# Float32r weights that begin 192 instead of 64 bytes past multiples of 256

## The chip, the cores and the metric

The kernel runs on one core of one Trainium2 chip. The metric is the device time of one execution in microseconds; less is better. A core has five engines with queues of their own: TensorE (PE in the profile; its weight loads are listed as PEld), VectorE (DVE), ScalarE (ACT), GpSimd (POOL) and SyncE (SP), which here only issues DMAs. On-chip memory (SBUF) has 128 partitions; "address" in this document always means the byte address within a partition, and "at 64" means that an operand begins 64 bytes past a multiple of 256.

## The reference

The input `x` is 8 x 3136 x 256. The reference takes the real part of a two-dimensional Fourier transform over the last two axes and puts a feed-forward block with a residual behind it:

```python
X = np.fft.fft(x, axis=1)
X = np.fft.fft(X, axis=2)
x = X.real.astype(np.float32)

mu = np.mean(x, axis=-1, keepdims=True)
var = np.mean((x - mu) ** 2, axis=-1, keepdims=True)
xn = (x - mu) / np.sqrt(var + 1e-06) * g_ln
ch = np.maximum(xn @ w_ch1, 0.0) @ w_ch2      # 256 -> 1024 -> 256
return (x + ch).astype(np.float32)
```

All data are float32.

## The kernel before

**The transform.** The sequence axis (3136 = 49 x 64) is transformed in two steps. `step1` (L247) multiplies folded input with a 64-point table; its result goes to a scratch buffer in device memory and comes back in another order (`store1`, `relayout`). `step2` (L299) multiplies the result, as weights, with tables `tab_s` as moving operand (L309, plain float32) and writes the pieces `ckh` and `ckl` of a chunk of 256 tokens (L330, L334). The transform over the last axis is folded into the first weight matrix, `w1`; only for the residual is it done explicitly (`residual`, L422, with weights from `ck` and the moving table `ty_s`, L428, plain float32).

**The feed-forward block.** It works chunk by chunk (`NCH` = 49 of them), and each chunk in eight steps of 128 hidden features. Step `s` has three parts, written out in this order in the main loop (L813 on): `moe1_b(s - 1)` makes the hidden activations' two pieces, `moe1_a(s)` the next hidden features, `moe2(s - 3)` adds the output of an earlier step.

**Products in three passes.** A float32 product is made of float32r products, which TensorE streams at one column a cycle: each operand is split into a high piece, rounded to float32r, and the rest. `PASSES` (L337) names the three products that count: high x low, low x high, high x high. `moe1_a` (L354) takes slices of `w1_hi` and `w1_lo` as weights (the stationary operand, 128 columns, loaded by a weight load ahead of each product) and `ckh`, `ckl` as moving operand (256 columns). `moe2` (L404) takes slices of `h_hi` and `h_lo` as weights and `w2_hi`, `w2_lo` as moving operand (256 columns). From the second batch on `step1` does the same with `t1_hi`, `t1_lo` as weights and `f_hi`, `f_lo` as moving operand (L262, 512 columns).

So one step of the loop is 6 products of `moe1_a` and 12 of `moe2`, each with a weight load of its own. TensorE can load the next weights while a product streams. Other products (L309, L428, L262, some small ones) come between steps, where the lists `after` and `late` (L606) put them. The order on TensorE, ScalarE, VectorE and GpSimd is that of the program text.

**Where operands lie.** Tiles get their addresses from pools, one after the other, in the order of the pools and of their tiles. The first pools are:

```python
moving.tile([128, 32], F32, name="margin")
w2_hi = moving.tile([128, 8, D], F32R, name="w2_hi")
w2_lo = moving.tile([128, 8, D], F32R, name="w2_lo")
weights.tile([128, 16], F32, name="offset")
w1_hi = weights.tile([128, 2, FF], F32R, name="w1_hi")
w1_lo = weights.tile([128, 2, FF], F32R, name="w1_lo")
```

`moving` holds the moving operands of all float32r products: `w2_hi`, `w2_lo`, `f_hi`, `f_lo`, `ck_hi`, `ck_lo`. Its tile `margin` is never used; it fills up to a multiple of 256 bytes, and the tiles behind it are multiples of 256 bytes long, so all of them begin at 0. `weights` holds the weights of float32r products (`w1_hi`, `w1_lo`, `t1_hi`, `t1_lo`, `h_hi`, `h_lo`) and two kinds of tiles that are weights of plain float32 products, `s2` (L309) and `ck` (L428). Its first tile, `offset`, isn't used either: its 16 elements make the rest begin at 64. These tiles too are multiples of 256 bytes long (`h_hi` and `ck` have 2304 bytes, 9 x 256), and the slices that become weights begin at multiples of 512 bytes within them. Exceptions: the second half of `ck` begins 1152 bytes into its tile, and one slice in the last chunk at element 120. Behind `weights` come the pools `const` (tables, the input `xs`) and `work` (everything that VectorE, ScalarE and GpSimd pass on); each start there is rounded up to 32 bytes.

Of the kernel before, what the change touches and what calls it, by code (L numbers as in the profile page):

```python
# [20 lines left out]
F32 = mybir.dt.float32  # L21
# [125 lines left out]
def tile_kernel(ctx: ExitStack, tc: tile.TileContext, x, g_ln, w1, w2, tu, tab, tz, ty, tw, out):  # L147
    nc = tc.nc
    moving = ctx.enter_context(tc.tile_pool(name="moving", bufs=1))
    weights = ctx.enter_context(tc.tile_pool(name="weights", bufs=1))  # L150
# [5 lines left out]
    moving.tile([128, 32], F32, name="margin")  # L156
    w2_hi = moving.tile([128, 8, D], F32R, name="w2_hi")
    w2_lo = moving.tile([128, 8, D], F32R, name="w2_lo")
    weights.tile([128, 16], F32, name="offset")
    w1_hi = weights.tile([128, 2, FF], F32R, name="w1_hi")  # L160
    w1_lo = weights.tile([128, 2, FF], F32R, name="w1_lo")
    t1_hi = weights.tile([128, 128], F32R, name="t1_hi")
# [683 lines left out]
```

## Time and profile before

| | us |
|---|---|
| median of 3 runs | 1007.62 (1007.08 to 1007.76) |
| the profiled execution | 1007.27 |
| its span, first to last instruction | 1005.5 |
| TensorE matmuls, busy | 995.1 |
| VectorE, busy | 812.3 |
| ScalarE, busy | 540.1 |
| GpSimd, busy | 243.9 |

The profile is of one execution. In its groups, a row gives line, engine, operation, output tile and input tiles, shapes and count; behind the bar stand busy time in us, the mean of one instruction in ns, and the idle time before these instructions with what ended it. Matmuls overlap: the next one starts long before the one before it has ended, so the sum of their durations isn't the time that they take, and the distance from start to start has to be read from the timeline. A row of the timeline gives the start in us from the span's start, the length in us, and the instruction. A row of the windows gives a stretch, its length, then busy time and number of instructions for PE, PEld, DVE, ACT and POOL, the granted clock, the DMA engines' share and GB/s.

### The profile page before, as it was taken

To read this page: it belongs to the slowest core of one execution; us is meant where nothing else is said; L and a number is where in the kernel's file an instruction comes from. 1 tells how busy PE (TensorE), PEld (TensorE's weight loads), DVE (VectorE), ACT (ScalarE), POOL (GpSimd) and SP (SyncE) were. 2 spreads that over 40 slices of the span, in tenths; PEclk is the share of its full clock that TensorE was granted. 3 is DMA by queue.
4 is the path that set the end of the run, shared out by engine and by line. 5 is a ranking of instruction groups with operands and counts; after the bars stand their busy time and mean duration, and the time that the engine had idled before them with its cause. 6 is when DMAs were issued, how large, how long until landed. Compare 5 with 4: busy or idle time off the path is not lost.

```text
span 1005.5 us, 21770 instructions
## 1 busy us (share of the span) xinstructions
PE 995.1 (99%) x8289; PEld 973.7 (97%) x8289; DVE 812.3 (81%) x2190; ACT 540.1 (54%) x1416; POOL 243.9 (24%) x278
## 2 busy tenths in 40 slices
PE   9999999999999999999999999999999999999998
PEld 6799999999999999999999999999999999999998
DVE  7788887878787788878877887878788788887887
ACT  3655556554555555655456555555555554555553
POOL 2146414530153203440054401532034300000000
PEclk9999999999999999999999999999999999999999
DMA  9933243223122511333132232224101230100101
GB/s 346 266 141 126 85 143 110 86 84 108 62 95 85 157 44 53 103 120 105 44 111 101 74 106 75 84 96 126 55 32 44 74 105 23 43 22 22 43 22 43
DMA packets 41528, 92.10 MB, mean 92 GB/s; under 512 B 4176, under 2 KB 18704, under 8 KB 40528
## 3 DMA queue, kind: packets, MB, share of 16 engines
q1 hardware_dynamic: 40016, 88.87, 27.1%
q8 instruction: 66, 1.08, 0.5%
q0 software_dynamic: 320, 1.05, 0.3%
q10 hardware_dynamic: 1088, 0.79, 0.2%
q14 instruction: 38, 0.31, 0.1%
HBM read 50.32 MB, written 40.37 MB: 90 GB/s over the span
## 4 chain that ended last, share of the span: by engine, by line
PE 88%; DVE 7%; ACT 2%; DMA 2%; issue 1%; SPq 0%; ACTq 0%; DVEq 0%
PE acc L404 49%; PE ab L354 25%; PE ps L309 5%; PE psy L428 4%; PE ps L262 3%; DVE h_lo L369 2%; DVE h L360 1%; DVE h L361 1%; ACT h_hi L368 1%; PE ps L255 1%; PE ps L257 1%; DMA scratch<-s 1%; DMA s<-scratch 1%; DMA xs<-x 0%; DVE st L450 0%
## 5 line engine op out<-in xcount | busy, mean ns | idle before, releaser
L404 PE MATMUL acc<-w_hi,h_lo 128*128 128x256 f32 x1568 | 437.1, 279 | 0.2 <-DVE h_lo L369 0.2
L404 PE MATMUL acc<-w_hi,h_hi 128*128 128x256 f32 x1568 | 436.9, 279 | 0.0
L404 PE MATMUL acc<-w_lo,h_hi 128*128 128x256 f32 x1568 | 436.9, 279 | 0.0
L369 DVE SCALAR_TENSOR_TENSOR h_lo<-h,h_hi 128x512 fp32r<-128x512 f32 x392 | 285.9, 729 | 160.8 <-ACT h_hi L368 159.0
L368 ACT ACTIVATE h_hi<-h 128x512 fp32r<-128x512 f32 x392 | 250.1, 638 | 266.0 <-DVE h L361 265.5
L404 PEld LDWEIGHTS acc<-w_hi,h_hi 128*128 128x128 f32 x1568 | 296.7, 189 | 0.0
L404 PEld LDWEIGHTS acc<-w_lo,h_hi 128*128 128x128 f32 x1568 | 295.3, 188 | 0.0
L404 PEld LDWEIGHTS acc<-w_hi,h_lo 128*128 128x128 f32 x1568 | 294.6, 188 | 0.6 <-DVE h_lo L369 0.4
L354 PE MATMUL ab<-ckl,w_hi 128*128 128x256 f32 x768 | 219.9, 286 | 2.6 <-DVE h L361 2.5
L354 PE MATMUL ab<-ckh,w_lo 128*128 128x256 f32 x768 | 214.5, 279 | 0.5 <-ACT ckh L330 0.3
L354 PE MATMUL ab<-ckh,w_hi 128*128 128x256 f32 x768 | 214.1, 279 | 0.0
L225 POOL TENSOR_TENSOR fl<-f,fh 128x512 fp32r<-128x512 f32 x49 | 64.2, 1309 | 495.5 <-ACT fh L219 489.3
L360 DVE TENSOR_TENSOR h<-asb,ab 128x256 f32<-128x256 f32 x384 | 158.7, 413 | 1.5 <-ACT asb L359 1.5
L361 DVE TENSOR_TENSOR h<-asb,ab 128x256 f32<-128x256 f32 x384 | 158.8, 414 | 0.0
L354 PEld LDWEIGHTS ab<-ckl,w_hi 128*128 128x128 f32 x768 | 144.3, 188 | 6.5 <-issue 2.1
L359 ACT COPY asb<-ab 128x256 f32<-128x256 f32 x384 | 139.0, 362 | 17.6 <-PE ab L354 13.9
L354 PEld LDWEIGHTS ab<-ckh,w_lo 128*128 128x128 f32 x768 | 144.7, 188 | 3.1 <-ACT ckh L330 0.5
L354 PEld LDWEIGHTS ab<-ckh,w_hi 128*128 128x128 f32 x768 | 145.3, 189 | 0.0
L330 ACT CAST ckh<-ps 128x392 fp32r<-128x392 f32 (+49 forms) x112 | 39.8, 356 | 62.3 <-PE ps L309 62.1
L265 ACT COPY s<-ps 128x508 f32<-128x508 f32 x56 | 32.8, 585 | 71.9 <-PE ps L262 58.7
L309 PE MATMUL ps<-tab_s,s 112*128 112x98 f32 (+1 forms) x512 | 65.6, 273 | 0.6 <-DMA s<-scratch 0.6
L309 PEld LDWEIGHTS ps<-tab_s,s 112*128 112x128 f32 x512 | 61.9, 191 | 1.1 <-PE pw L670 1.1
(108 smaller groups left out, 964.8 us busy)
## 6 DMA issues: line engine op xcount, KB each, us to landing
xs<-x SPq DMA_DIRECT2D x56, 512.0 KB, 4.4
out<-o SPq DMA_DIRECT2D x96, 256.0 KB, 3.0
scratch<-s SPq DMA_DIRECT2D x49, 256.0 KB, 2.2
s<-scratch SPq DMA_DIRECT2D x7, 1792.0 KB, 9.7
w1p_all<-w SPq DMA_DIRECT2D x8, 512.0 KB, 8.7
scratch<-s POOLq DMA_DIRECT2D x4, 256.0 KB, 6.3
s<-scratch SPq DMA_DIRECT2D x2, 448.0 KB, 5.8
s<-scratch SPq DMA_DIRECT2D x1, 896.0 KB, 12.2
```

What stands on the lines that cost most here:

```text
L225: nc.gpsimd.tensor_tensor(out=lo, in0=f, in1=hi.bitcast(F32), op=ALU.subtract)
L265: nc.scalar.copy(s[:, :, :, :127], ps[:, :, :, :127])
L309: nc.tensor.matmul(ps[:, h, k0 - base:k1 - base], s2[b][:KP, g, 128 * h:128 * h + 128], tab_s[:, h, k0:k1], start=(h == 0 and g == 2 * j), ...
L330: nc.scalar.copy(hi, src)
L354: nc.tensor.matmul(pt, wt[wi][:, j, fs], ch[xi][:, j, :w], start=(n == 0), stop=(n == 2))
L359: nc.scalar.copy(asb[:, :w], pa)
L360: nc.vector.tensor_tensor(out=h[:, :w], in0=asb[:, :w], in1=pb, op=ALU.add)
L361: nc.vector.tensor_tensor(out=h[:, w:], in0=asb[:, :m], in1=pb[:, :m], op=ALU.subtract)
L368: nc.scalar.activation(h_hi, h, AF.Relu)
L369: nc.vector.scalar_tensor_tensor(out=h_lo, in0=h, scalar=0.0, in1=h_hi.bitcast(F32), op0=ALU.max, op1=ALU.subtract)
L404: nc.tensor.matmul(acc[c, i][:, side], hs[xi][:, h0:h0 + 128], ws[wi][:, f], start=(f == 0 and side == 0 and n == 0), stop=(f == 7 and n = ...
L428: nc.tensor.matmul(ps[:, j, :129 + j], ck[:, j], ty_s[:, j, :129 + j], start=(j == 0), stop=True, skip_group_check=True)
```

## The change

The unused first tile of the pool `weights` grows from 16 to 48 elements, from 64 to 192 bytes. Every tile behind it moves up by 128 bytes: those of `weights`, `const` and `work`. The pool `moving` lies ahead of it and stays. So the weights of float32r products begin at 192 instead of 64 while their moving operands stay at 0; instructions, their order, waits and transfers are the same.

```diff
     w2_lo = moving.tile([128, 8, D], F32R, name="w2_lo")
-    weights.tile([128, 16], F32, name="offset")
+    weights.tile([128, 48], F32, name="offset")
     w1_hi = weights.tile([128, 2, FF], F32R, name="w1_hi")
```

## The prediction

> **What bounds the kernel now.** I read the page from the top: busy times, the clock row, the chain that ended last, then the groups of TensorE.
>
> ```profile
> span 1005.5 us, 21770 instructions
> ## 1 busy us (share of the span) xinstructions
> PE 995.1 (99%) x8289; PEld 973.7 (97%) x8289; DVE 812.3 (81%) x2190; ACT 540.1 (54%) x1416; POOL 243.9 (24%) x278
> ...
> PEclk9999999999999999999999999999999999999999
> ...
> PE 88%; DVE 7%; ACT 2%; DMA 2%; issue 1%; SPq 0%; ACTq 0%; DVEq 0%
> ```
>
> TensorE is busy for 99% of the span at the full granted clock, and 88% of the chain is its matmuls. Nothing else is close, so the time is the number of products times the distance from one to the next, plus the little that is left. What counts are the float32r products of `moe2` (L404) and `moe1_a` (L354):
>
> ```profile
> L404 PE MATMUL acc<-w_hi,h_lo 128*128 128x256 f32 x1568 | 437.1, 279 | 0.2 <-DVE h_lo L369 0.2
> L404 PE MATMUL acc<-w_hi,h_hi 128*128 128x256 f32 x1568 | 436.9, 279 | 0.0
> L404 PE MATMUL acc<-w_lo,h_hi 128*128 128x256 f32 x1568 | 436.9, 279 | 0.0
> ...
> L354 PE MATMUL ab<-ckl,w_hi 128*128 128x256 f32 x768 | 219.9, 286 | 2.6 <-DVE h L361 2.5
> L354 PE MATMUL ab<-ckh,w_lo 128*128 128x256 f32 x768 | 214.5, 279 | 0.5 <-ACT ckh L330 0.3
> L354 PE MATMUL ab<-ckh,w_hi 128*128 128x256 f32 x768 | 214.1, 279 | 0.0
> ```
>
> That is 4704 + 2304 = 7008 products of 256 columns. Their 279 ns is a mean of overlapping instructions, so the distance has to come from start times, and those show that 279 is no product's time. The timeline of TensorE has long unbroken stretches, of two kinds. First and last product of one stretch of each kind, with the groups and windows inside them:
>
> ```profile
> 233.69 0.28 PE L354 MATMUL ab<-ckh,w_lo 128*128 128x256 f32 x1
> ...
> 250.41 0.28 PE L404 MATMUL acc<-w_hi,h_hi 128*128 128x256 f32 x1
> ```
>
> ```profile
> 252.68 0.28 PE L354 MATMUL ab<-ckl,w_hi 128*128 128x256 f32 x1
> ...
> 268.54 0.28 PE L404 MATMUL acc<-w_hi,h_hi 128*128 128x256 f32 x1
> ```
>
> ```profile
> L404 PE MATMUL acc<-w_hi,h_lo 128*128 128x256 f32 x31 | 8.7, 281 | 0.0
> ...
> L404 PEld LDWEIGHTS acc<-w_hi,h_hi 128*128 128x128 f32 x31 | 6.0, 192 | 0.0
> L404 PEld LDWEIGHTS acc<-w_hi,h_lo 128*128 128x128 f32 x31 | 5.8, 188 | 0.0
> ```
>
> ```profile
> L404 PE MATMUL acc<-w_hi,h_lo 128*128 128x256 f32 x31 | 8.6, 276 | 0.0
> ...
> L404 PEld LDWEIGHTS acc<-w_hi,h_lo 128*128 128x128 f32 x31 | 5.8, 188 | 0.0
> ```
>
> ```profile
> 234.00:250.00 16.00, 16.00 (x138) 16.00 (x137) 14.42 (x41) 8.37 (x21) 0.00 (x0) 1.00 0.06 23
> 253.00:268.00 15.00, 15.00 (x135) 15.00 (x134) 13.67 (x40) 8.03 (x21) 0.95 (x1) 1.00 0.05 20
> ```
>
> From 233.69 to 250.41 lie 142 steps: 16.72 / 142 = **117.7 ns**. From 252.68 to 268.54 lie 140: 15.86 / 140 = **113.3 ns**. Same instructions, same addresses, clock 1.00, no idle time in either. In the slow stretch every product takes 281 ns and every third weight load 192; in the fast one they take 276 and 188. So each stretch runs in one of two rhythms, 4.4 ns apart, and the mean of 279 says how often: with 437.0 / 1568 = 278.7 ns, L404 is slow in (278.7 - 276) / (281 - 276) = 0.54 of its products. I take 0.54 for L354 too (its last two rows, 279.3 and 278.8, give 0.66 and 0.56, restarts included). That makes 3780 slow and 3230 fast products.
>
> What switches the rhythm is another kind of product in between, such as the three of L262, 512 columns wide. Here it goes from 113 to 118 ns:
>
> ```profile
> 206.67 0.28 PE L404 MATMUL acc<-w_lo,h_hi 128*128 128x256 f32 x1
> 206.78 0.28 PE L404 MATMUL acc<-w_hi,h_hi 128*128 128x256 f32 x1
> 206.90 0.39 PE L262 MATMUL ps<-fl,t_hi 128*128 128x512 f32 x1
> ...
> 207.71 0.28 PE L354 MATMUL ab<-ckh,w_lo 128*128 128x256 f32 x1
> 207.83 0.28 PE L354 MATMUL ab<-ckh,w_hi 128*128 128x256 f32 x1
> 207.94 0.28 PE L354 MATMUL ab<-ckl,w_hi 128*128 128x256 f32 x1
> 208.06 0.28 PE L354 MATMUL ab<-ckh,w_lo 128*128 128x256 f32 x1
> ```
>
> **The change, part by part.** It adds no instruction, wait or transfer and takes none away. Everything from `w1_hi` on moves by 128 bytes in each partition.
>
> *The engines other than TensorE.* Operands of VectorE, ScalarE, GpSimd and the DMAs shift by half of 256. The four `h` buffers lie 2112 = 8 x 256 + 64 bytes apart, so they already begin at four different remainders, and the sums that write them one after the other take the same:
>
> ```profile
> 253.77 0.41 DVE L360 TENSOR_TENSOR h<-asb,ab 128x256 f32<-128x256 f32 x1
> 255.82 0.41 DVE L360 TENSOR_TENSOR h<-asb,ab 128x256 f32<-128x256 f32 x1
> 258.14 0.41 DVE L360 TENSOR_TENSOR h<-asb,ab 128x256 f32<-128x256 f32 x1
> 260.67 0.41 DVE L360 TENSOR_TENSOR h<-asb,ab 128x256 f32<-128x256 f32 x1
> ```
>
> I cost them at 0. They are covered besides: VectorE, the busiest of them, has 1.3 of 15 us free in the fast window. Without that cover, a longer VectorE operation would be paid once per step of the loop.
>
> *Plain float32 products* (L309, L428, L255). Their weights and moving operands lie in the pools `weights`, `const` and `work`, which all move together, so the distance between the two operands is as before. Cost 0.
>
> *Float32r products.* Here the weights move and the moving operands do not: the distance goes from 64 to 192. The loads take as many columns and their count stays. The question is only what the load of the next weights does to the stream of the running product. The trace has two products of the fast rhythm during which weights from elsewhere are loaded. For L586 it is `minus`: `weights` is a multiple of 256 long, so `const` begins at 64; with each start rounded up to 32 bytes, `tu_s` (1552 bytes), `tab_s` (12552), `tz_s` (200) and `tw_all` (2560) put `minus` at 96. For the second it is the residual's slice of `ck` in the last chunk that begins at element 120 (L425): 64 + 480 bytes, a remainder of 32.
>
> ```profile
> L354 PE MATMUL ab<-ckl,w_hi 128*128 128x256 f32 x1 | 0.3, 282 | 0.0
> L354 PE MATMUL ab<-ckh,w_lo 128*128 128x256 f32 x1 | 0.3, 276 | 0.0
> ...
> L586 PEld LDWEIGHTS psw<-w_hi,minus 128*128 128x128 f32 x1 | 0.2, 188 | 0.0
> ```
>
> ```profile
> L404 PE MATMUL acc<-w_hi,h_hi 128*128 128x256 f32 x1 | 0.3, 280 | 0.0
> L404 PE MATMUL acc<-w_hi,h_lo 128*128 128x256 f32 x1 | 0.3, 276 | 0.0
> ...
> L428 PEld LDWEIGHTS psy<-ty_s,ck 128*128 128x128 f32 x1 | 0.2, 187 | 0.0
> ```
>
> The first row of each fence is the product beside that load: 282 ns at 96 and 280 at 32, after 276 for its neighbours with loads from 64. So the place of the weights does matter, at a grain of 32 bytes: one step to either side costs 4 to 6 ns, which is the slow rhythm's 281.
>
> The Trainium skill ("SBUF — State Buffer", section "Who interferes with whom") gives TensorE two independent read ports, one for the moving operand and one for weights, and has it wait for nobody; by that the change costs nothing and the time stays at 1007.3 us. The 280 and 282 ns rows contradict its reason, so I don't rest the forecast on it.
>
> For 192 itself no float32r row exists. Bounds from the nearest rows: at best all 7008 products run at 113.3 ns, 3780 x 4.4 = 16.6 us less; at worst all run at 117.7, as the rows at 32 and 96 suggest for a bad place, 3230 x 4.4 = 14.2 us more. I take 0, for two reasons. A product streams 256 elements while 128 weights are read, so the moving stream passes 256 bytes while the weights pass 128: a pattern of boundaries every 256 bytes on the moving side looks the same again when the weights move by 128. And 32 and 96, which are 64 apart, behave alike, which fits a period of 64 or 128 bytes; 128 is a multiple of both. The one place where weights lie at 192 now, the second half of `ck` (1152 = 4.5 x 256 bytes on), fits too, though its product is plain float32: L428, half of whose loads are from 64 and half from 192, has the mean of L309, all from 64.
>
> ```profile
> L309 PEld LDWEIGHTS ps<-tab_s,s 112*128 112x128 f32 x512 | 61.9, 191 | 1.1 <-PE pw L670 1.1
> L428 PEld LDWEIGHTS psy<-ty_s,ck 128*128 128x128 f32 x396 | 48.4, 191 | 0.3 <-DVE o L479 0.3
> ```
>
> Sum: 0 us against the profiled execution's 1007.27 (its span 1005.5 and 1.8 around it). The median of the three runs, 1007.62, is 0.03% above it; I give 1007.5.
>
> **The rivals.**
>
> 1. *The rhythm is always, or more often, the fast one.* The rhythm is decided anew at every stage boundary by the phase in which the next load meets the stream, and half of 256 bytes may turn that phase. For it: the switch after L262 shows that a few nanoseconds decide. Against it: nothing shows 192 as the better side. Price: 3780 x 4.4 = 16.6 us, down to 990.7; half of it 999. VectorE doesn't stop it: in the fast window it is busy 13.67 of 15.00 us and TensorE still has no idle time.
> 2. *The rhythm is always, or more often, the slow one* (slower). The load from 192 meets the stream in every product, as those from 32 and 96 do. The place is L404 and L354, the price 3230 x 4.4 = 14.2 us, up to 1021.5; it decides the sign as soon as the slow share rises by 2 / (7008 x 0.0044) = 0.065, to over 0.60. For it: two of the places that the trace shows beside 64 are bad. Against it: both are odd multiples of 32, and 192 is not.
> 3. *The change doesn't do what it says*, because the pool rounds the larger tile away. But 64 and 192 bytes are both multiples of the 32 to which starts are rounded, so everything behind moves by exactly 128. I give it no chance; the time would be my forecast's.
>
> **How the numbers follow.** A period that divides 128 bytes: chance 0.34, change 0. Otherwise the share of slow stretches is drawn anew, with little to say to which side: 0.08 that it lands within 2 us of now, 0.28 for rival 1 and 0.30 for rival 2, a little more for 2 because a place picked anew has two bad neighbours in the trace and one good. Two microseconds are 0.2%, about what a measurement of this kernel can tell from no change. So: same 0.42, faster 0.28, slower 0.30. The likeliest case is no change, 1007.5 us, by itself 1005.5 to 1009.5. As both rivals have natural ends (every stretch fast, every stretch slow), the range goes to these: 990 to 1022. What it leaves out, a third rhythm beyond either, I put under 0.15.
>
> **What would show it.** Right: L404 keeps a mean near 278.7 ns, the timeline has the same two steps of 113.3 and 117.7, and stretches change at the same stage boundaries. Rival 1: L404 at 276 to 277, no weight load of 192 ns in a window of 15 us. Rival 2: L404 at 280 to 281 and the same 192 ns on every third load throughout. Wrong in a way I don't foresee: a step that is neither (below 113, or above 118), or the gain or loss in rows other than L404 and L354: idle time before them, or longer operations of VectorE, where 128 bytes would have cost something after all.

## The result and the profile after

| | us | ratio to before (95% interval) |
|---|---|---|
| before, 4 runs | 1007.35 (1006.25 to 1007.76) | |
| after, 4 runs | 1020.63 (1020.40 to 1022.55) | 1.0138 [1.012, 1.0155] |
| profiled execution after | 1020.47 (span 1018.7) | |

The changed kernel is 1.4% slower, 13.3 us. (Of the executions behind this document, one, the profiled one with weights at 32, ran at a granted clock of 0.557 and took 1657.4 us, and its time and steps are left out below.) The page of the kernel after, busy times, clock, chain and TensorE's groups:

```profile
span 1018.7 us, 21770 instructions
...
PE 1008.5 (99%) x8289; PEld 987.1 (97%) x8289; DVE 811.4 (80%) x2190; ACT 540.4 (53%) x1416; POOL 243.3 (24%) x278
...
PEclk9999999999999999999999999999999999999999
...
PE 89%; DVE 7%; ACT 2%; DMA 1%; issue 1%; ACTq 0%; SPq 0%; DVEq 0%
...
L404 PE MATMUL acc<-w_hi,h_hi 128*128 128x256 f32 x1568 | 438.2, 279 | 0.0
L404 PE MATMUL acc<-w_lo,h_hi 128*128 128x256 f32 x1568 | 438.1, 279 | 0.0
L404 PE MATMUL acc<-w_hi,h_lo 128*128 128x256 f32 x1568 | 437.6, 279 | 0.1
...
L354 PE MATMUL ab<-ckh,w_lo 128*128 128x256 f32 x768 | 215.0, 280 | 0.5 <-ACT ckh L330 0.4
```

The span grew by 13.2 us and TensorE's busy time by 13.4. VectorE, ScalarE and GpSimd are where they were (811.4 after 812.3, 540.4 after 540.1, 243.3 after 243.9), and the clock is full. So the time came from TensorE alone. But the groups hardly show it: the three rows of L404 grew by about 1 us each and still have a mean of 279 ns. These products overlap, and the length of one isn't its share of the time. The distance from start to start is. First and last product of one stretch in the timeline of after, 142 steps apart, and the groups and the window inside it:

```profile
235.23 0.28 PE L354 MATMUL ab<-ckh,w_lo 128*128 128x256 f32 x1
...
251.95 0.28 PE L404 MATMUL acc<-w_hi,h_hi 128*128 128x256 f32 x1
```

```profile
L404 PE MATMUL acc<-w_lo,h_hi 128*128 128x256 f32 x29 | 8.1, 280 | 0.0
L404 PE MATMUL acc<-w_hi,h_lo 128*128 128x256 f32 x29 | 8.1, 279 | 0.0
...
L404 PEld LDWEIGHTS acc<-w_hi,h_lo 128*128 128x128 f32 x29 | 5.5, 188 | 0.0
...
L404 PEld LDWEIGHTS acc<-w_hi,h_hi 128*128 128x128 f32 x29 | 5.4, 187 | 0.0
```

```profile
236.00:251.00 15.00, 15.00 (x129) 15.00 (x129) 13.84 (x40) 7.71 (x20) 0.00 (x0) 1.00 0.06 20
```

16.72 / 142 = **117.7 ns**, the step of the slow rhythm of before, with no idle time in TensorE. The record of each instruction is a little different from before's slow stretches: 279 to 280 ns for every product instead of 281, and no load of 192 ns. The same 117.7 ns can thus stand behind two sets of lengths.

The fast rhythm has not gone, though. Early in the same execution lies a stretch of 53 steps, again with the groups inside it:

```profile
79.03 0.28 PE L354 MATMUL ab<-ckl,w_hi 128*128 128x256 f32 x1
...
85.04 0.28 PE L404 MATMUL acc<-w_hi,h_hi 128*128 128x256 f32 x1
```

```profile
L404 PE MATMUL acc<-w_hi,h_hi 128*128 128x256 f32 x10 | 2.8, 276 | 0.0
...
L404 PEld LDWEIGHTS acc<-w_hi,h_hi 128*128 128x128 f32 x10 | 1.9, 188 | 0.0
```

6.01 / 53 = **113.4 ns**, 276 and 188 ns: the fast rhythm of before, with every weight load from 192. So a load from 192 doesn't cost anything in itself. What changed is how the stream gets into one rhythm and out of it. The last place before 970 us where the changed kernel leaves the fast one:

```profile
111.68 0.28 PE L404 MATMUL acc<-w_lo,h_hi 128*128 128x256 f32 x1
111.79 0.28 PE L404 MATMUL acc<-w_hi,h_hi 128*128 128x256 f32 x1
111.91 1.03 PE L309 MATMUL ps<-tab_s,s 112*128 112x98 f32 x8
112.78 1.08 PE L428 MATMUL psy<-ty_s,ck 128*128 128x129 f32 x8
113.61 0.36 PE L354 MATMUL ab<-ckl,w_hi 128*128 128x256 f32 x1
113.81 0.28 PE L354 MATMUL ab<-ckh,w_lo 128*128 128x256 f32 x1
113.93 0.28 PE L354 MATMUL ab<-ckh,w_hi 128*128 128x256 f32 x1
114.05 0.28 PE L354 MATMUL ab<-ckl,w_hi 128*128 128x256 f32 x1
```

and one of the places where it could go back and doesn't (in before, the same three products of L262 change the rhythm nearly every time):

```profile
207.81 0.28 PE L404 MATMUL acc<-w_lo,h_hi 128*128 128x256 f32 x1
207.93 0.28 PE L404 MATMUL acc<-w_hi,h_hi 128*128 128x256 f32 x1
208.05 0.40 PE L262 MATMUL ps<-fl,t_hi 128*128 128x512 f32 x1
...
208.75 0.28 PE L354 MATMUL ab<-ckl,w_hi 128*128 128x256 f32 x1
208.87 0.28 PE L354 MATMUL ab<-ckh,w_lo 128*128 128x256 f32 x1
208.99 0.28 PE L354 MATMUL ab<-ckh,w_hi 128*128 128x256 f32 x1
```

I read the start times of all products between 100 and 970 us in this way and counted what the two commonest kinds of other products do between two stretches of the stream (steps up to 115 ns are fast, those from 116 to 121 slow; blocks that hold still other products are left out):

| between two stretches | before, all at 64 | after, all at 192 |
|---|---|---|
| L262, stream fast ahead of it | 19 of 20 go slow | none (one at 85 us stays fast) |
| L262, stream slow ahead of it | 25 of 25 go fast | 1 of 45 goes fast |
| L309 and L428, fast ahead | 15 of 15 go slow | 1 of 1 goes slow |
| L309 and L428, slow ahead | 7 of 21 go fast | 0 of 35 go fast |
| inside a stretch | no change | no change |

With all weights at 64, L262 toggles the rhythm, and somewhat under half of all steps are fast (0.47). With all at 192, the one time that the stream is fast ahead of L309 and L428 it goes slow, and next to nothing leads out: 0.02 of the steps are fast. The mean step of the 256-column products goes from 115.74 to 117.72 ns, and 1.98 ns x 6,813 pairs is 13.5 us, against 13.2 of the span.

### The profile page after: what moved, and what is told of

Read it like the earlier page. It is cut to its first block, busy times and chain, and to the rows that moved or that the text cites. A ratio compares the mean times of both kernels' runs of the same rounds, so it can differ in the third digit from the quotient of the medians.

```text
span 1018.7 us, 21770 instructions
## 1 busy us (share of the span) xinstructions
PE 1008.5 (99%) x8289; PEld 987.1 (97%) x8289; DVE 811.4 (80%) x2190; ACT 540.4 (53%) x1416; POOL 243.3 (24%) x278
## 4 chain that ended last, share of the span: by engine, by line
PE 89%; DVE 7%; ACT 2%; DMA 1%; issue 1%; ACTq 0%; SPq 0%; DVEq 0%
PE acc L404 49%; PE ab L354 25%; PE ps L309 5%; PE psy L428 4%; PE ps L262 3%; DVE h_lo L369 2%; DVE h L360 1%; DVE h L361 1%; ACT h_hi L368 1%; PE ps L255 1%; PE pw L670 1%; PE ps L257 1%; DMA scratch<-s 1%; DMA s<-scratch 0%; DVE st L450 0%
## 5 line engine op out<-in xcount | busy, mean ns | idle before, releaser
L404 PE MATMUL acc<-w_hi,h_hi 128*128 128x256 f32 x1568 | 438.2, 279 | 0.0
L404 PE MATMUL acc<-w_lo,h_hi 128*128 128x256 f32 x1568 | 438.1, 279 | 0.0
L404 PE MATMUL acc<-w_hi,h_lo 128*128 128x256 f32 x1568 | 437.6, 279 | 0.1
L404 PEld LDWEIGHTS acc<-w_lo,h_hi 128*128 128x128 f32 x1568 | 294.5, 188 | 0.0
L404 PEld LDWEIGHTS acc<-w_hi,h_lo 128*128 128x128 f32 x1568 | 294.0, 187 | 0.5 <-DVE h_lo L369 0.3
L404 PEld LDWEIGHTS acc<-w_hi,h_hi 128*128 128x128 f32 x1568 | 293.8, 187 | 0.0
L309 PE MATMUL ps<-tab_s,s 112*128 112x98 f32 (+1 forms) x512 | 65.6, 273 | 1.0 <-DMA s<-scratch 1.0
L309 PEld LDWEIGHTS ps<-tab_s,s 112*128 112x128 f32 x512 | 62.0, 191 | 1.5 <-PE pw L670 1.5
```

Source lines behind the costliest of these rows:

```text
L309: nc.tensor.matmul(ps[:, h, k0 - base:k1 - base], s2[b][:KP, g, 128 * h:128 * h + 128], tab_s[:, h, k0:k1], start=(h == 0 and g == 2 * j), ...
L404: nc.tensor.matmul(acc[c, i][:, side], hs[xi][:, h0:h0 + 128], ws[wi][:, f], start=(f == 0 and side == 0 and n == 0), stop=(f == 7 and n = ...
```

## The experiments

Two theories at the outset. **The place**: what a load costs depends on how far its weights lie from the moving operand, and a load from 192 meets the stream in every product. **The rhythm**: the place decides only which rhythm the stream falls into at a boundary. All ratios are to the kernel before, run on the same chip (medians 1006.93 to 1007.52). Mean steps and shares of fast steps are worked out from the start times of all products.

**Is it the distance?** Against the kernel before, the moving operands go up instead of the weights being placed anew; weights, tables and the other engines' operands then lie as they do after.

```diff
-    moving.tile([128, 32], F32, name="margin")
+    moving.tile([128, 64], F32, name="margin")
```

> Weights at 192 as in the changed kernel, but the moving operands at 128 too, so the distance between them is 64 as before; the pools const and work lie as in the changed kernel. Theory 1 (only the distance of weights and moving operand counts): 1007.5 us, both rhythms present, 281 and 276 ns. Theory 2 (the weights' own place in 256 bytes counts): 1020.5, one rhythm of 117.8 ns. Theory 3 (the shift of const and work, that is of the other engines' operands, counts): 1020.5.

1007.65 us, 1.0008 [0.9998, 1.0017]. The row of L404 can't tell it from the changed kernel (279 ns in both), but the steps do: their mean is 115.69 ns and 0.48 of them are fast, after 115.74 and 0.47 in before, and L262 toggles again.

Weights at 192 with moving operands at 128 behave like 64 and 0. In this pair the distance counts, and the shift of all other operands is worth nothing that can be told.

**What is the period?** Against the changed kernel, the tile `offset` in seven other sizes; each distance is four times the number of elements.

```diff
-    weights.tile([128, 48], F32, name="offset")
+    weights.tile([128, 80], F32, name="offset")
```

> Weights 320 = 256 + 64 bytes past, moving operands at 0. If the pattern repeats every 256 bytes, theories 1 and 2 alike give 1007.5 us with 0.5 to 0.55 of the L404 products at 281 ns. If a longer block counts (512), another time, 1007.5 being no more likely than 1020.5.

```diff
-    weights.tile([128, 48], F32, name="offset")
+    weights.tile([128, 64], F32, name="offset")
```

> Weights and moving operands both at multiples of 256. Theories 1 and 2 say nothing of the place itself; the period of 128 that the prediction rested on has fallen, so 0 need not equal 128. If the load from the place of the stream is the worst one, every step is at least 117.8 ns and the time at least 1020.5 us; if a place other than 64 can hold the fast rhythm throughout, 991.

```diff
-    weights.tile([128, 48], F32, name="offset")
+    weights.tile([128, 32], F32, name="offset")
```

> Weights at 128, half way. With a pattern symmetrical about 128 (the load ahead of the stream or behind it), 64 and 192 would have been equal, and they are not; so nothing binds 128 to either. Slow throughout gives 1020.5 us, fast throughout 991, a mixture lies between. A step that is neither 113.3 nor 117.8 ns would show that there are more than two rhythms.

```diff
-    weights.tile([128, 48], F32, name="offset")
+    weights.tile([128, 8], F32, name="offset")
```

> Weights at 32. The trace of before has one product beside a load from 32: 280 ns, the slow rhythm's length. Theory A (that row was the place's doing): every step near 118 ns or more, 1020 to 1028 us. Theory B (the row was the phase's doing, at the edge between two kinds of product): like its neighbours 0 and 64, something between 1007 and 1034, with the 113.3 ns rhythm still there.

```diff
-    weights.tile([128, 48], F32, name="offset")
+    weights.tile([128, 24], F32, name="offset")
```

> Weights at 96, with the one row of 282 ns in the trace of before. Theory A: every step near 118 to 120 ns, 1020 to 1034 us. Theory B: between 1007 and 1028, with the 113.3 ns rhythm still there.

```diff
-    weights.tile([128, 48], F32, name="offset")
+    weights.tile([128, 40], F32, name="offset")
```

> Weights at 160, between 128 (1027.8 us) and 192 (1020.5). If the time is a smooth function of the distance, 1021 to 1028. If a place at an odd multiple of 32 has a cost of its own, more than 1028.

```diff
-    weights.tile([128, 48], F32, name="offset")
+    weights.tile([128, 56], F32, name="offset")
```

> Weights at 224, between 192 (1020.5 us) and 256, which is 0 (1033.9). Smooth: 1021 to 1034. A cost of its own at odd multiples of 32: more than 1034. A fast rhythm, as at 64: under 1015, which neither neighbour suggests.

| distance, bytes | us | ratio | mean step, ns |
|---|---|---|---|
| 256 (0) | 1033.87 | 1.0278 [1.0255, 1.0302] | 119.83 |
| 32 (three runs) | 1024.24 | 1.0166 [1.0149, 1.0183] | not read |
| 64, before | 1007.35 | | 115.74 |
| 96 | 1024.01 | 1.0165 [1.0148, 1.0182] | 118.21 |
| 128 | 1027.76 | 1.0204 [1.0187, 1.0221] | 118.82 |
| 160 | 1036.12 | 1.0285 [1.0270, 1.0301] | 119.96 |
| 192, after | 1020.63 | 1.0138 [1.0120, 1.0155] | 117.72 |
| 224 | 1015.00 | 1.0077 [1.0062, 1.0092] | 116.89 |
| 320 (64) | 1007.34 | 1.0004 [0.9995, 1.0013] | 115.67 |

320 is 64 again, and no two distances 128 apart agree: 32 and 160 are 11.9 us apart, 96 and 224 are 9.0. The period is not 128; a period of 256 fits, though only this one pair 256 apart was measured. The time doesn't go smoothly with the distance either: 160 is slower than its neighbours 128 and 192, and 224 is faster than its neighbours 192 and 256. The two rhythms are not all there is. At 0, TensorE's groups give

```profile
L404 PE MATMUL acc<-w_hi,h_lo 128*128 128x256 f32 x1568 | 443.9, 283 | 0.1
...
L404 PEld LDWEIGHTS acc<-w_hi,h_hi 128*128 128x128 f32 x1568 | 300.9, 192 | 0.0
```

with steps around 120 ns throughout and 191 to 192 ns for the loads of every product. At 128 and 160 steps of 115 to 125 ns alternate, and at 224 there are regular patterns, one of 116 and 117 ns and one from 113 to 120. At 0, 96, 128, 160 and 224 no more than two steps of 115 ns or less follow each other anywhere, while before has up to 141 and after up to 53. The time follows the mean step in each: 1007.35 us plus (step - 115.74) x 6.81 gives 1036.1 at 160, 1024.2 at 96, 1015.2 at 224 and, furthest from the measured time, 1035.2 at 0.

**Which weights pay?** If a load from 192 costs something where it stands, moving only `h` (two thirds of the loads) or only `w1` (one third) should cost about that share. Against the kernel before, with `h`, `s2` and `ck` at 192 and `w1`, `t1` at 64:

```diff
     t1_lo = weights.tile([128, 128], F32R, name="t1_lo")
+    weights.tile([128, 32], F32, name="offset_h")
```

> Only what lies behind t1_lo moves: the hidden activations are loaded from 192, w1 and t1 from 64. If a product pays for the load that runs beside it, the 4704 products of moe2 go from a mean step of 115.6 to 117.8 ns: 10 us more, 1017 us; those of moe1_a, 2304, may go either way with the phase in which they are entered: 1011 to 1021. If the place of w1 made the whole change: 1007.5.

Against the changed kernel, with `w1` and `t1` at 192 and `h`, `s2`, `ck` at 64:

```diff
     t1_lo = weights.tile([128, 128], F32R, name="t1_lo")
+    weights.tile([128, 32], F32, name="offset_h")
```

> The mirror of the run before: w1 and t1 are loaded from 192, the hidden activations from 64. Products of moe1_a from 115.9 to 117.8 ns: 2304 x 1.9 = 4 us more, 1012 us, with moe2 free to follow either rhythm: 1005 to 1021. If the two parts of the change add up, this one's and the last one's differences to before make 13.3 us together; if the rhythm is one state of the whole stream, either part alone can break it, and they make more.

998.63 us, 0.9914 [0.9896, 0.9932], and 996.80 us, 0.9895 [0.988, 0.9911]. Either half of the change makes the kernel *faster*, though both together make it slower, and both times lie below every time that was expected. That ends the first theory. In the first kernel the loads of `moe2` come from 192 and 0.77 of all steps are fast. What is new is that the rhythm changes inside the stream. The timeline of the second kernel (all lines are one further down):

```profile
233.83 0.28 PE L405 MATMUL acc<-w_hi,h_hi 128*128 128x256 f32 x1
233.96 0.28 PE L355 MATMUL ab<-ckl,w_hi 128*128 128x256 f32 x1
234.07 0.28 PE L355 MATMUL ab<-ckh,w_lo 128*128 128x256 f32 x1
...
234.54 0.28 PE L355 MATMUL ab<-ckh,w_hi 128*128 128x256 f32 x1
234.66 0.28 PE L405 MATMUL acc<-w_hi,h_lo 128*128 128x256 f32 x1
234.77 0.28 PE L405 MATMUL acc<-w_lo,h_hi 128*128 128x256 f32 x1
234.89 0.28 PE L405 MATMUL acc<-w_hi,h_hi 128*128 128x256 f32 x1
235.00 0.28 PE L405 MATMUL acc<-w_hi,h_lo 128*128 128x256 f32 x1
235.11 0.28 PE L405 MATMUL acc<-w_lo,h_hi 128*128 128x256 f32 x1
```

From `moe1_a` on L355, weights at 192, 117 to 118 ns from one to the next; at the passage to `moe2` (L405), weights at 64, it becomes 113 (from 234.66 to 235.11 four steps take 0.45) and stays for 119 steps. Over the whole execution this kernel has 57 places where four slow steps are followed by four fast ones, and in 53 of them the step in which the weights go from 192 to 64 is the last slow or the first fast one; the first kernel has 76, all of that kind. Before has one, after none. In the first kernel L262 leads from fast to slow 44 times of 45, and it is faster all the same: the stream has a way out.

**One tile in two.** Against the kernel before, every second `h_lo` buffer at 192 (a scratch tile of the same tag gets the same size):

```diff
-        h_lo = weights.tile([128, n], F32R, tag="h_lo", name=f"h_lo{s}", bufs=4)
+        h_lo = weights.tile([128, n + 32], F32R, tag="h_lo", name=f"h_lo{s}", bufs=4)[:, :n]
...
-            e = weights.tile([128, 512], F32, tag="h_lo", name=f"e{key}", bufs=4)
+            e = weights.tile([128, 544], F32, tag="h_lo", name=f"e{key}", bufs=4)[:, :512]
```

> The four buffers of h_lo lie at 64, 192, 64, 192; all other weights stay at 64. In moe2 the h_lo piece is loaded while the product high x high streams, and is then the weights of low x high. If a product pays for the load beside it, the product ahead (w_hi,h_hi) is the one whose step is longer, in the steps of the loop whose h_lo is at 192; if it pays for the place of its own weights, it is w_hi,h_lo. Time between 1005 and 1020.5 us.

1001.60 us, 0.9945 [0.9927, 0.9963], 0.68 of the steps fast; this too is below the range expected. It was to tell whether the product beside a load from 192 pays or the product that uses these weights. Neither does: within `moe2`, steps from an `h_hi` at 64 to an `h_lo` at 192 take 113.4 ns on average, 1% of them slow. Its question has no answer, since nothing is paid there. It has 55 changes from slow to fast inside the stream, 45 of them at 192 to 64.

**Is it `t1`, the weights of L262?** L262 toggles at 64 and keeps the slow rhythm at 192, so its own weights could decide. Three kernels, beside four from above in the table. `t1` alone at 192, against before:

```diff
+    weights.tile([128, 32], F32, name="offset_t")
     t1_hi = weights.tile([128, 128], F32R, name="t1_hi")
     t1_lo = weights.tile([128, 128], F32R, name="t1_lo")
+    weights.tile([128, 32], F32, name="offset_r")
```

> Only t1_hi and t1_lo move to 192: the weights of 147 products of 512 columns, 33 us in all, whose own steps change by 0.2 us at most (231.8 against 232.9 ns on average). If the rhythm of a stretch is set by the phase in which it is entered, the time may still move by several us, up to 16.6 down or 14.2 up, with the slow share of the 256-column products changed and no new step length. If places act only through the products that load them, 1007.5.

`t1` alone at 64, against after:

```diff
+    weights.tile([128, 32], F32, name="offset_t")
     t1_hi = weights.tile([128, 128], F32R, name="t1_hi")
     t1_lo = weights.tile([128, 128], F32R, name="t1_lo")
+    weights.tile([128, 32], F32, name="offset_r")
```

> The changed kernel with t1_hi and t1_lo alone back at 64. If the place of t1 decides whether L262 changes the rhythm, slow stretches become fast at about every second L262 again: 1003 to 1012 us, both rhythms in the timeline. If the place of the stream's own weights decides, slow throughout: 1020.5.

Only `w1` at 192, the rest at 64 with `t1`, against after:

```diff
+    weights.tile([128, 32], F32, name="offset_t")
     t1_hi = weights.tile([128, 128], F32R, name="t1_hi")
```

> w1 at 192, hidden activations at 64 as in the run w_192 (996.8 us), but t1 at 64. If the place of t1 decides, L262 leads from the fast rhythm into the slow one again (it did so 44 times with w1 and t1 at 64, hidden activations at 192), until the next change from 192 to 64 leads out: 998 to 1001 us. If not, 996.8.

| kernel | `w1` | `t1` | `h` | us | ratio | what L262 does |
|---|---|---|---|---|---|---|
| before | 64 | 64 | 64 | 1007.35 | | toggles (44 of 45) |
| `t1` at 192 | 64 | 192 | 64 | 1007.24 | 1.0003 [0.9993, 1.0012] | keeps: 25 fast, 20 slow |
| after | 192 | 192 | 192 | 1020.63 | 1.0138 [1.0120, 1.0155] | keeps slow (44 of 45) |
| `t1` at 64 | 192 | 64 | 192 | 1020.64 | 1.0133 [1.0118, 1.0149] | keeps slow (44 of 45) |
| `w1` at 192 | 192 | 64 | 64 | 997.60 | 0.9902 [0.9885, 0.9918] | fast to slow (44 of 45) |
| `w1`, `t1` at 192 | 192 | 192 | 64 | 996.80 | 0.9895 [0.9880, 0.9911] | keeps fast (44 of 45) |
| `h` at 192 | 64 | 64 | 192 | 998.63 | 0.9914 [0.9896, 0.9932] | fast to slow (44 of 45) |

Where the stream is fast ahead of L262, the place of `t1` decides, with single exceptions, in the five kernels of the table that show it: at 64 the stream goes slow, at 192 it stays fast. With `w1` alone at 192 this is easily missed, because the slow rhythm lasts only for the six products of `moe1_a`. The first and the seventh product behind an L262 (L263 there), with `t1` at 64 and then with `t1` at 192:

```profile
569.86 0.28 PE L355 MATMUL ab<-ckl,w_hi 128*128 128x256 f32 x1
...
570.56 0.28 PE L405 MATMUL acc<-w_hi,h_lo 128*128 128x256 f32 x1
```

```profile
569.10 0.28 PE L355 MATMUL ab<-ckl,w_hi 128*128 128x256 f32 x1
...
569.78 0.28 PE L405 MATMUL acc<-w_hi,h_lo 128*128 128x256 f32 x1
```

To the nanosecond the six steps take 706 and 680 ns, 117.7 and 113.3 each. At the passage to `moe2`, from 192 to 64, the first of the two is fast again. This is the course that was expected if `t1` decides; the time, 997.60 us, came out just below the 998 to 1001 that went with it, and its interval overlaps that of 996.80.

Where the stream is slow ahead, `t1` alone doesn't decide. At 192 it keeps the slow rhythm (20 of 20 with `t1` alone there, 44 of 45 in after); at 64 it leads out of it in before (25 of 25), and doesn't with `w1` and `h` at 192 (44 of 45 keep slow). Both rhythms can come out of an L262 whose weights lie at either place, and in neither pair of kernels that differ in `t1` alone, the first two rows and the next two, does the time change.

**A way out in every group of three.** If weights going from 192 to 64 end the slow rhythm, the change should be put where it comes often: between the three passes of `moe1_a`. Against after, `w1_hi` and `t1` at 192, `w1_lo`, `h`, `s2`, `ck` at 64:

```diff
     w1_hi = weights.tile([128, 2, FF], F32R, name="w1_hi")
+    weights.tile([128, 32], F32, name="offset_lo")
     w1_lo = weights.tile([128, 2, FF], F32R, name="w1_lo")
+    weights.tile([128, 32], F32, name="offset_t")
     t1_hi = weights.tile([128, 128], F32R, name="t1_hi")
     t1_lo = weights.tile([128, 128], F32R, name="t1_lo")
+    weights.tile([128, 32], F32, name="offset_r")
```

> Only w1_hi and t1 at 192; w1_lo and all others at 64. Each group of three products then has a change from 192 to 64 within it. If that change ends the slow rhythm, a slow stretch lasts a few products instead of 16 to 24, the slow share falls under 0.08 and the time to 992 to 995 us. If a change of place has a price of its own in every group (2304 products, up to 4 ns each), 997 to 1004.

Against before, `w1_lo` and `t1` at 192, the rest at 64:

```diff
     w1_hi = weights.tile([128, 2, FF], F32R, name="w1_hi")
+    weights.tile([128, 32], F32, name="offset_lo")
     w1_lo = weights.tile([128, 2, FF], F32R, name="w1_lo")
     t1_hi = weights.tile([128, 128], F32R, name="t1_hi")
     t1_lo = weights.tile([128, 128], F32R, name="t1_lo")
+    weights.tile([128, 32], F32, name="offset_r")
```

> The other way round: w1_lo and t1 at 192, w1_hi and all others at 64. The same change from 192 to 64 in every group: 992 to 995 us if that ends the slow rhythm whichever piece it is, 1003 to 1012 if it needs a longer run at 192 ahead of it.

**993.02 us**, 0.9857 [0.9842, 0.9872], and 995.04 us, 0.9876 [0.9861, 0.9891]: both faster than either kernel of the change. The page of the first (lines three further down) and its timeline after a stage of L312 and L431, which are L309 and L428 of before:

```profile
span 991.0 us, 21770 instructions
...
L407 PE MATMUL acc<-w_hi,h_lo 128*128 128x256 f32 x1568 | 433.2, 276 | 0.2 <-DVE h_lo L372 0.2
L407 PE MATMUL acc<-w_lo,h_hi 128*128 128x256 f32 x1568 | 433.0, 276 | 0.0
```

```profile
230.59 1.08 PE L431 MATMUL psy<-ty_s,ck 128*128 128x129 f32 x8
231.43 0.36 PE L357 MATMUL ab<-ckl,w_hi 128*128 128x256 f32 x1
231.63 0.28 PE L357 MATMUL ab<-ckh,w_lo 128*128 128x256 f32 x1
231.75 0.28 PE L357 MATMUL ab<-ckh,w_hi 128*128 128x256 f32 x1
231.87 0.28 PE L357 MATMUL ab<-ckl,w_hi 128*128 128x256 f32 x1
231.98 0.28 PE L357 MATMUL ab<-ckh,w_lo 128*128 128x256 f32 x1
232.09 0.28 PE L357 MATMUL ab<-ckh,w_hi 128*128 128x256 f32 x1
```

Where the kernel after goes on at 118 ns, the three steps from 231.75 to 232.09 take 0.34 here: 113 ns from the third product on. This kernel goes on fast after 38 of 38 such stages and 44 of 45 blocks of L262 (its `t1` is at 192, which keeps the fast rhythm there); 0.96 of its steps are fast, the mean is 113.54 ns. In one step of the loop the weights go from 192 to 64 three times here, twice with `w1_lo` at 192, once with all of `w1` or all of `h` there, never before and after: 993.0, 995.0, 996.8 to 998.6, 1007.4 and 1020.6 us. That order fits the passage as the way out. A mere count of passages isn't the rule, however: the kernel with every second `h_lo` at 192 has two of them a step on average and takes 1001.6.

## Why the prediction was wrong

- **What bounds the kernel**: right. The difference lies in the distance of TensorE's 256-column products, in two rhythms. By start times 0.53 of the steps before are slow, for the 0.54 that was worked out from the mean of L404.
- **Other engines at 0, plain float32 products at 0**: right. With the distance kept, the same shift of their operands changes nothing that can be told (1.0008).
- **Float32r products at 0**: this is the step that failed, and with it the forecast. It rested on "a pattern of boundaries every 256 bytes on the moving side looks the same again when the weights move by 128", a period of 128 bytes. The scan has none: each of the four pairs 128 apart differs by 6 us or more. The argument counted bytes on paths that no row showed. Its second leg, that 32 and 96 behave alike, is true of the times (1024.2 and 1024.0), but two points of a pattern don't give its period: 160 and 224, as far apart, differ by 21 us. The third, from the equal 191 ns of the loads of L309 and L428, compared plain float32 products, and there only lengths of loads, which don't show a product's distance.
- **Rival 2, always the slow rhythm**: its price was right. 3230 x 4.4 = 14.2 us, measured 13.3, as 0.02 of the steps are still fast. Its mechanism, "the load from 192 meets the stream in every product, as those from 32 and 96 do", was wrong: the fast stretch at 79 us and the kernel with `h` at 192 have such loads at 113 ns. Its sign, 192 ns on every third load, didn't come either; the slow rhythm at 192 has loads of 188.
- **Rival 1, the rhythm "decided anew at every stage boundary"**: this was the right mechanism, with the wrong sign for this change. What it takes was stated too loosely: boundaries don't draw a rhythm by chance but mostly repeat one answer (25 of 25, 44 of 45), so a change of the place moves the share of slow steps far, not a little. Its price for all fast, 990.7 us, is nearly what `w1_hi` at 192 reaches (993.0).
- **L404's mean as a witness**: it was to tell 278.7 from 280 to 281. It came out at 279 with the slow rhythm throughout. The lengths of overlapping products are not calibrated against the step once the place changes.

What is shown, for eight distances within 256 bytes, is that the distance decides which steps the stream takes, that with all weights at 192 almost nothing leads out of the slow rhythm, and that the stream leaves it by itself in the mixes tried, nearly always where weights go from 192 to 64 (174 of 188 places in the three kernels counted). What inside the chip makes the rhythms was not observed, nor why L262 with `t1` at 64 leads out of the slow rhythm in the kernel before and not with `w1` and `h` at 192, nor why 192 to 64 ends the slow rhythm, and not at every such passage. These stay open.

## What to carry to other kernels

Where TensorE is busy all the time with overlapping products, as here, take its cost from the distance between starts, and look for more than one distance: a share of slow steps is time that no row of idle time shows. The place of weights against the moving operand is then worth a scan in steps of 32 bytes, with several places among the operands of one loop too, because the best single place (1007.3 us) was beaten by a mix (993.0). Before you argue a period from symmetry, measure one more point of it.

## What the runs showed of the hardware

Identical instructions in the same order took from 993.0 to 1036.1 us, 4.3%, by where weights lie alone. The Trainium skill ("SBUF — State Buffer", section "Who interferes with whom") gives the moving operand and the weight loads ports of their own, independent of each other, and says that only the port pair shared by VectorE and GpSimd causes contention. The runs differ from that: moving both operands by 128 bytes leaves the time (1.0008) and moving only the weights doesn't (1.0138), so loading weights and streaming are not independent here, whatever joins them; the measurement decides.

The rhythm is a state that lasts. With all weights at 64 or all at 192, stretches of up to 142 steps keep it (one change in the whole of before, none after); other products between, or weights from another place, change it. It isn't chance from run to run either: the four runs of the kernel with `w1_hi` at 192 lie within 0.9 us of each other.
